# Attention on the needed key blocks only (bands, gathered sampled blocks, shared first and last block), values in 32-column tiles, and a new planner

## The chip, the cores and the metric

The kernel runs on one core of one Trainium2 chip. The metric is device time in microseconds (us) of the slowest core, here of the only one. Runs are compared with runs of the kernel before on the same chip. The engines are called TensorE (PE in the profile, PEld for its weight loads), VectorE (DVE), ScalarE (ACT), GpSimd (POOL) and SyncE (SP).

## The reference

Inputs are q, k and v of 4 batches, 8 heads, 768 positions and 64 columns, a table `sampled_blocks` of 24 x 3 block numbers (the same for all batches and heads), and the weights of a gated network.

```python
# attention, blocks of 32 positions: 24 blocks
mask = |block_i - block_j| <= 1  or  block_i or block_j is the first or the last
mask |= key block is one of the three sampled blocks of the query block
x = softmax(where(mask, q k^T / 8, -1e9)) v           # per batch and head
# network: x is [4, 768, 512], w_in [512, 1024], conv_w [3, 1024], w_out [1024, 512]
h = relu(x @ w_in)
c = conv_w[0] * h[t-1] + conv_w[1] * h[t] + conv_w[2] * h[t+1]
out = (h * sigmoid(c)) @ w_out
```

## The kernel before

The kernel before computes all 768 keys for each query. The mask is 24 more rows in the product of Q and K (64 + 24 = 88 rows). A unit is 1024 columns of scores: one exponential and eight value products of 128 x 128 by 65 columns. There are 144 units.

```python
def s_fn(e, ...):                       # scores of a unit, mask rows inside the product
    nc.tensor.matmul(out=st[:, 128 * x:128 * (x + n_)],
                     lhsT=QK[kc % 2][s][0:88, 1, hh, kc // 2, :],
                     rhs=QK[par][s][0:88, 0, hh, idx:idx + n_, :]..., start=True, stop=True)
def e_fn(e, ...):
    nc.scalar.activation(out=pt_t[ptb.index], in_=st_t[stb.index], func=AF.Exp, bias=0.0, scale=0.125)
def a_fn(e, ...):                       # four of these, twice a unit
    nc.tensor.matmul(out=o[:, off:off + 65], lhsT=pt_t[ptb.index][:, 128 * x:128 * x + 128],
                     rhs=VT[P % NSLOT][:, hh, kc, 0:65], ...)
# ... the gated network of a half batch (384 positions): ReLU mostly on VectorE, edges copied on GpSimd,
#     three taps and two adds per 768 columns on VectorE, tanh on ScalarE, then the gate on VectorE
for o in sc.run():                      # a list scheduler in the kernel sets each engine's order from assumed costs
    ...
```

This scheduler (the planner, below) sets the order of each engine's instructions. In a later run, with the new planner, another order of the same work took 10.6 us more (e_alt).

The softmax here doesn't subtract the row's maximum and nothing guards it: scores larger than these inputs give would overflow.

## Time and profile before

| kernel before | |
|---|---|
| time | 276.06 us (median of 2 runs, 276.02 to 276.1) |
| busy: TensorE, VectorE, ScalarE | 213.5, 201.4, 168.9 us |
| first convolution tap on VectorE | 61.0 us after the start |
| VectorE busy before it, and in the 215.2 us after it | 22.9 and 178.5 us (83%) |
| transfers of instructions for TensorE (queue 8) | 19 of 16 KB |

"Busy" is the time in which at least one instruction of that engine runs, waits left out. VectorE, busy 73% of the whole time, is busy for 18.9 of the 20 us from 120 to 140 us, so the span is read by stage.

### The profile page before, as it was taken

What the parts mean: (1) busy time and instruction counts of PE and PEld (TensorE: products, weight loads), DVE (VectorE), ACT (ScalarE), POOL (GpSimd) and SP (SyncE); (2) the same over time, 40 slices, a digit from 0 to 9 for tenths busy, and PEclk for the clock granted to TensorE, in tenths of its full rate; (3) what the DMA queues carried; (4) which work ended last, traced back from release to release, by engine and by line L of the source; (5) the groups of instructions that cost most, each with busy time, mean ns of one, the idle gap of its engine ahead of it and who ended that gap; (6) DMA issues with size and microseconds to landing.
All of it is one profiled execution on the core that took longest, in us unless ns stands there. A gap on an engine that the chain in (4) does not pass through costs nothing.

```text
span 276.2 us, 6428 instructions
## 1 busy us (share of the span) xinstructions
PE 213.5 (77%) x2503; PEld 152.0 (55%) x2521; DVE 201.4 (73%) x545; ACT 168.9 (61%) x189; POOL 72.1 (26%) x171
## 2 busy tenths in 40 slices
PE   5724499459779887997779769979898799749573
PEld 1523488337657655676557545766675567524221
DVE  6713362037997998399959994999799749986984
ACT  1511289517786887387858784887788747830420
POOL 8722331211223453022434410211112002211500
PEclk9555599959999999999999999999999999986868
DMA  6999999984215999963599964722200131011003
GB/s 141 141 211 197 160 157 116 159 154 113 55 30 120 148 167 166 230 166 64 78 180 179 168 88 157 140 64 45 93 17 15 31 129 40 18 28 76 1 0 152
DMA packets 67778, 30.35 MB, mean 110 GB/s; under 512 B 60868, under 2 KB 62916, under 8 KB 67748
## 3 DMA queue, kind: packets, MB, share of 16 engines
q0 software_dynamic: 25856, 11.14, 35.7%
q1 hardware_dynamic: 41892, 18.80, 31.6%
q8 instruction: 19, 0.31, 0.5%
q14 instruction: 11, 0.09, 0.1%
HBM read 23.08 MB, written 6.29 MB: 106 GB/s over the span
## 4 chain that ended last, share of the span: by engine, by line
DVE 53%; PE 20%; DMA 16%; issue 4%; SPq 3%; POOL 2%; ACT 1%; DVEq 0%; ACTq 0%
DVE m L710 17%; DVE m L718 10%; DVE hE L683 8%; DMA vn<-in_v_dram 7%; DMA xT<-xtok 6%; DVE gT L737 6%; PE mix L671 6%; PE mix L640 6%; DVE xtok L542 4%; PE st L578 4%; DVE tn L734 4%; PE av L610 2%; DMA et<-nat 2%; SPq L493 2%; PE st L640 1%
## 5 line engine op out<-in xcount | busy, mean ns | idle before, releaser
L587 ACT ACTIVATE pt<-st 128x1024 bf16<-128x1024 f32 x144 | 140.7, 1025 | 69.2 <-PE st L578 68.7
L671 PE MATMUL mix<-xT,winb 128*128 128x384 bf16 x256 | 53.9, 341 | 13.5 <-DMA xT<-xtok 8.6
L610 PE MATMUL av<-vt,pt 128*128 128x65 bf16 x1152 | 60.0, 195 | 0.2 <-ACT pt L587 0.2
L610 PEld LDWEIGHTS <-pt 128*128 128x128 bf16 x1152 | 52.4, 99 | 12.5 <-issue 8.7
L640 PE MATMUL mix<-woutb,gT 128*128 128x512 bf16 x143 | 41.8, 386 | 19.6 <-DVE gT L737 14.3
L710 DVE TENSOR_SCALAR m<-hE,cw 128x384 bf16<-128x384 bf16 x192 | 56.3, 348 | 0.3 <-POOL hE L702 0.3
L683 DVE TENSOR_SCALAR hE<-mix 128x384 bf16<-128x384 f32 x58 | 32.0, 552 | 26.8 <-PE mix L671 26.4
L578 PE MATMUL st<-et,ot 88*128 88x128 bf16 (+1 forms) x224 | 43.9, 240 | 1.3 <-ACT pt L587 0.9
L578 PE MATMUL st<-ot 88*128 88x128 bf16 (+1 forms) x224 | 43.6, 238 | 0.7 <-ACT pt L587 0.5
L578 PE MATMUL st<-et 88*128 88x128 bf16 (+1 forms) x208 | 43.4, 249 | 0.9 <-ACT pt L587 0.2
L578 PE MATMUL st<-ot,et 88*128 88x128 bf16 (+1 forms) x208 | 42.8, 246 | 1.5 <-ACT pt L587 0.7
L578 PEld LDWEIGHTS <-ot 88*128 88x128 bf16 x448 | 35.9, 100 | 13.6 <-issue 3.5
L696 POOL COPY hE<-hE 128x254 bf16<-128x254 bf16 x32 | 13.3, 415 | 111.3 <-DVE hE L683 93.8
L578 PEld LDWEIGHTS <-et 88*128 88x128 bf16 x416 | 33.4, 100 | 11.6 <-issue 2.9
L640 PEld LDWEIGHTS <-gT 128*128 128x128 bf16 x192 | 15.9, 101 | 42.6 <-DVE gT L737 25.5
L718 DVE TENSOR_TENSOR m<-m 128x768 bf16<-128x768 bf16 x64 | 35.6, 557 | 1.0
L731 ACT ACTIVATE tn<-m 128x768 bf16<-128x768 bf16 x32 | 26.9, 840 | 14.3 <-DVE m L718 14.1
L671 PEld LDWEIGHTS <-winb 128*128 128x128 bf16 x256 | 23.7, 101 | 19.3 <-issue 9.7
L650 DVE COPY o2s<-mix 128x512 f32<-128x512 f32 x20 | 13.4, 689 | 12.5 <-PE mix L640 12.5
L737 DVE TENSOR_TENSOR gT<-tn,hE 128x768 bf16<-128x768 bf16 x32 | 18.0, 563 | 1.1
L542 DVE TENSOR_TENSOR xtok<-av,rcp 128x384 bf16<-128x384 f32 x32 | 17.8, 558 | 1.1
L413 POOL DMA_DIRECT2D nat<-in_q_dram x15 | 11.4, 757 | 26.2 <-PE mix L450 17.7
(67 smaller groups left out, 129.2 us busy)
## 6 DMA issues: line engine op xcount, KB each, us to landing
out_dram<-o2s SPq DMA_DIRECT2D x24, 256.0 KB
vn<-in_v_dram POOLq DMA_DIRECT2D x16, 192.0 KB, 5.8
nat<-in_q_dram POOLq DMA_DIRECT2D x15, 192.0 KB, 4.8
nat<-in_k_dram POOLq DMA_DIRECT2D x15, 192.0 KB, 6.2
ot<-et SPq DMA_DIRECT2D x12, 192.0 KB
winb<-in_moe_w_in_dram POOLq DMA_DIRECT2D x1, 1024.0 KB, 12.9
woutb<-in_moe_w_out_dram POOLq DMA_DIRECT2D x1, 1024.0 KB, 17.9
et<-msk SPq DMA_DIRECT2D x12, 72.0 KB
```

The costliest lines, as they stand in the source:

```text
L542: nc.vector.tensor_tensor(out=xtok_t[xk.index].rearrange("p c h d -> p h c d"), in0=o[:, :, :, 0:64], in1=rcp.unsqueeze(3).broadcast_to([1 ...
L578: nc.tensor.matmul(out=st[:, 128 * x:128 * (x + n_)], lhsT=QK[kc % 2][s][0:88, 1, hh, kc // 2, :], rhs=QK[par][s][0:88, 0, hh, idx:idx + n ...
L587: nc.scalar.activation(out=pt_t[ptb.index], in_=st_t[stb.index], func=AF.Exp, bias=0.0, scale=0.125)
L610: nc.tensor.matmul(out=o[:, off:off + 65], lhsT=pt_t[ptb.index][:, 128 * x:128 * x + 128], rhs=VT[P % NSLOT][:, hh, kc, 0:65], start=(y in ...
L640: nc.tensor.matmul(out=acc(0), lhsT=gT_t[gb.index][:, ffc, 128 * c:128 * c + 128], rhs=woutb[:, ffc, :], start=(ffc == 0), stop=(ffc == NF ...
L650: nc.vector.tensor_copy(out=o2s_t[ob.index], in_=acc(0))
L671: nc.tensor.matmul(out=mix_t[hb.index][:, 0:384], lhsT=winb[:, fc, 128 * ffc:128 * ffc + 128], rhs=xT_t[xt_buf[n].index][:, fc, :], start= ...
L683: nc.vector.tensor_scalar(out=dst, in0=mix_t[hb.index][:, 0:384], scalar1=0.5, scalar2=0.0, op0=ALU.mult, op1=ALU.max)
L710: nc.vector.tensor_scalar(out=m_t[cb.index][:, x, y], in0=hE_t[heb.index][:, f0 + y, 128 * x:128 * x + 384], scalar1=cw[:, x, f0 + y:f0 + ...
L718: nc.vector.tensor_tensor(out=m[:, a_], in0=m[:, a_], in1=m[:, b_], op=ALU.add)
L731: th = op({"ACT": t_act(768)}, lambda e, cb=cb: nc.scalar.activation(out=tn_t[cb.index], in_=m_t[cb.index][:, 1], func=AF.Tanh, bias=0.0, ...
L737: g2 = op({"DVE": t_d2(768)}, lambda e, cb=cb, gtb=gtb, heb=heb, f0=f0: nc.vector.tensor_tensor(out=gT_t[gtb.index][:, f0:f0 + 2, :], in0= ...
```

## The change

The intent: compute only what the mask keeps. For a pair of heads and half a batch, the scores are now bands of 128 keys around each query block (384 + 320 columns), the first and last block for all (736 columns, with the full row of the block that sees everything), and the three sampled blocks of each query block (704 columns). For the sampled blocks K is gathered by copies on VectorE and V by transfers from a scratch tensor in memory. Values are 67 products per pair, each 32 columns wide. The convolution runs on a width of 768 without copied edges. The planner is new: it runs a forward and a backward pass six times and keeps the best order by its own costs.

The core of the diff (1,600 lines, cut):

```diff
-                                 lhsT=QK[kc % 2][s][0:88, 1, hh, kc // 2, :],
-        nc.scalar.activation(out=pt_t[ptb.index], in_=st_t[stb.index], func=AF.Exp, bias=0.0, scale=0.125)
...
+            for a in range(lo, lo + cnt, 6):                       # 6 blocks: 18 registers, then 5: 15
+                _, vals = nc.values_load_multi_w_load_instructions(
+                    off_i[0:1]...[:, 3 * (i0 + a):3 * (i0 + z)], engines=[eng], ...)
+                rv[(n, name)] += list(vals)
+        rl = op({"DVE": 0.5}, loads(EN.DVE, "DVE", 0, NX), due - 5, [blk] + list(prev_copies))
+        for x in range(NX):                                        # NX = 11 query blocks of the half
+            def cp(e, x=x):
+                for s in range(3):
+                    nc.vector.tensor_copy(out=dst[:, :, x, 32 * s:32 * s + 32],
+                                          in_=KT[...][:, :, bass.ds(rv[(n, "DVE")][3 * x + s], 32)])
+            o = op({"DVE": 0.40}, cp, ...)
...
+            vg_w[n].append(op({"POOL": 1.25}, lambda e, x=x: nc.gpsimd.indirect_dma_start(...)))   # 6 blocks
+        rs = op({"SP": 0.5}, loads(EN.SP, "SP", NIX, NX - NIX), due - 3, [blk] + list(prev_sp))
+                    nc.sync.dma_start(out=VG[...], in_=vs_t[b][bass.ds(rv[(n, "SP")][...], 32), :])  # 5 x 3
...
+                        nc.tensor.matmul(out=dst, lhsT=l_, rhs=r_, ...)          # 67 a pair, dst 32 rows
+        ao = op({"PE": 0.72}, a_fn, ...)
...
+    for x in range(passes):                                        # planner: forward and backward, 6 passes
+            order, span = self.forward(prio, x == 0)
```

The number in braces is what the planner believes the operation to cost.

## The prediction

> **What bounds the kernel now.** I read the page first: the totals of the engines, the slices, and the shares of the chain that ended last.
>
> ```profile
> PE 213.5 (77%) x2503; PEld 152.0 (55%) x2521; DVE 201.4 (73%) x545; ACT 168.9 (61%) x189; POOL 72.1 (26%) x171
> ...
> PE   5724499459779887997779769979898799749573
> ...
> DVE  6713362037997998399959994999799749986984
> ACT  1511289517786887387858784887788747830420
> ...
> DMA  6999999984215999963599964722200131011003
> ...
> DMA packets 67778, 30.35 MB, mean 110 GB/s; under 512 B 60868, under 2 KB 62916, under 8 KB 67748
> ...
> DVE 53%; PE 20%; DMA 16%; issue 4%; SPq 3%; POOL 2%; ACT 1%; DVEq 0%; ACTq 0%
> ```
>
> No engine is full over the whole span. A slice is 6.9 us. In the first eight slices the DMA digit is 9 while PE, DVE and ACT are mostly below 5; from slice nine DVE is at 7 to 9, and in the last four ACT has nothing left. So I cut the span into stages with the view of busy time in stretches (columns: length, then busy time of PE, weight load, DVE, ACT, POOL, then clock, DMA share, GB/s):
>
> ```profile
> 0.00:40.00 40.00, 22.98 (x223) 16.98 (x224) 19.21 (x59) 13.56 (x15) 18.64 (x31) 0.66 1.25 168
> 40.00:60.00 20.00, 12.31 (x182) 9.82 (x179) 3.24 (x9) 12.11 (x14) 3.08 (x4) 0.89 1.20 142
> 60.00:245.00 185.00, 158.61 (x2038) 117.58 (x2054) 156.04 (x420) 137.11 (x151) 45.21 (x123) 0.99 0.59 103
> 245.00:276.20 31.20, 19.57 (x68) 7.60 (x68) 22.93 (x59) 6.17 (x10) 5.13 (x13) 0.75 0.15 54
> ```
>
> The first 60 us wait for transfers. The middle, 185 us, has PE at 86%, DVE at 84% and ACT at 74%: three engines nearly in balance. The last 31 us are the gated network of the last half with no attention beside it. Then the costly groups and, for what an instruction costs back to back, two stretches of the order of time:
>
> ```profile
> L587 ACT ACTIVATE pt<-st 128x1024 bf16<-128x1024 f32 x144 | 140.7, 1025 | 69.2 <-PE st L578 68.7
> L610 PE MATMUL av<-vt,pt 128*128 128x65 bf16 x1152 | 60.0, 195 | 0.2 <-ACT pt L587 0.2
> L710 DVE TENSOR_SCALAR m<-hE,cw 128x384 bf16<-128x384 bf16 x192 | 56.3, 348 | 0.3 <-POOL hE L702 0.3
> L683 DVE TENSOR_SCALAR hE<-mix 128x384 bf16<-128x384 f32 x58 | 32.0, 552 | 26.8 <-PE mix L671 26.4
> L718 DVE TENSOR_TENSOR m<-m 128x768 bf16<-128x768 bf16 x64 | 35.6, 557 | 1.0
> ```
> ```profile
> 35.51 16.61 ACT L587 ACTIVATE pt<-st 128x1024 bf16<-128x1024 f32 x18 [1.22 <-PE st L578]
> ```
> ```profile
> 66.96 1.46 DVE L710 TENSOR_SCALAR m<-hE,cw 128x384 bf16<-128x384 bf16 x6
> 68.34 0.55 DVE L718 TENSOR_TENSOR m<-m 128x768 bf16<-128x768 bf16 x1
> 68.81 0.35 DVE L734 TENSOR_SCALAR tn<-tn 128x768 bf16<-128x768 bf16 x1
> ```
>
> Durations overlap, so I count in pitches, start to start: an exponential 16.61/18 = 0.923 us, a convolution tap (68.34-66.96)/6 = 0.23, an add of 768 columns 68.81-68.34 = 0.47. Eight value products fill 0.41 us in the same view, (0.41-0.195)/7 = 0.031 us each. A first-layer matmul of 384 columns comes to 0.16, an output matmul of 512 to 0.217, a ReLU on DVE to 0.47. Summed so, before needs about 133 + 27 us on ACT, 185 on DVE and 185 on PE (scores 63, values 36, first layer 42, output 42).
>
> [...]
>
> **The change, part by part.**
>
> *Scores and exponentials.* Before computes all 768 keys for each query with the mask as 24 more rows; after computes per head pair and half 384 + 320 (bands), 736 (first and last block), 704 (sampled). These are 2144 columns in four exponentials. At 0.07 + n/1200 us (0.923 - 1024/1200 = 0.07) that is 4 x 0.07 + 1.79 = 2.07 us, times 32 = 66 us against 133. ACT then takes over 59 ReLUs of 64 (0.39 each, 23 us), 32 evictions of transposed Q and K (0.71, 23 us) and 16 output copies (8 us); tanh stays at 32 x 0.71 = 23. ACT: about 143 us against 160. The 67 us off the exponentials are largely spent again.
>
> *PE.* Scores: 28 products of 64 columns at 0.031 and four of 128 to 224 at 0.056 and 0.096: 1.17 us, times 32 = 37 against 63. Values: 67 products in 32-column tiles per pair, 2144 in all. If four run together but their loads do not hide, I put a pair at 1.0 us (an estimate: half of 67 x 0.031), so 32 against 36. New: 512 transposes at about 0.04 = 20. Layers as before, 84. Sum 173 against 185[...].
>
> *DVE.* Removed: 53 of 58 ReLUs (25 us), 16 of 24 output copies (10), copies of V (6). Taps: 96 at 0.23 plus 48 double ones at 0.33 = 38 against 44. Adds, +1, gates and normalisation about the same (30 + 9 + 16 + 22). Evictions 8 each way. Added: 264 copies of 128 columns that gather the sampled K blocks, each with a register instruction in front. The smallest DVE operations in the trace take 0.16 to 0.19 us; I put one at 0.15 to 0.20, so 40 to 53 us. Start-up tables and memsets 12 us. Sum: 181 to 195 against 185. DVE, already 53% of the chain, gets no relief at all.
>
> *Transfers.* Gone: 24 transposing transfers of Q and K, the 12 + 12 shuffles to the odd copies and the mask rows. Loads become pieces of 2 KB where before they were 768 B in and 384 B out. Added: V goes to a scratch tensor in memory (3.2 MB), comes back twice (6 MB), and gathers read 1040 B rows, about 8.8 MB. More bytes, but few small packets; at 50 ns for some 31,000 packets (before: 0.316 x 16 x 276 / 41,892 = 33 ns for 450 B) that is about 100 us of the sixteen engines, under half the span.
>
> *POOL.* The edge copies of hE (28 us) go; 48 gathers of perhaps 1.2 us and rearranging V come. No bound.
>
> *Sum by stage.* Start: a first batch of 4.7 MB at some 200 GB/s lands by about 24 us, V's round trip ends about 5 us later, so values begin near 28 us; the order of DVE puts the first tap only behind twelve normalisations and 132 gather copies, near 48 us, with about 45 us of DVE work done. Left: about 143 us (188 - 45). Where before's DVE was bound it reached 18.9 of 20 us; at 90% this is 159 us, so the last DVE work is near 207. The planner's bursts will collide with gathers and PSUM buffers (two of each kind, as before): I add 12 us. Tail: output matmuls, copies and the last write after DVE, 5 us (before: 269 to 276). 207 + 12 + 5 = 224. So the gain is not from the bound engine doing less, but from filling it: 60 us of start become about 45, and the middle goes from 84% towards 90%.
>
> **The rivals.**
>
> *Column tiles do not overlap.* Then 67 x 0.031 = 2.1 us per pair, 66 us[...]: end near 250. For it: [...] 4136 load and matmul pairs must be issued. [...]
>
> *Gather copies are dearer.* A register operation before each and an address from a register could make 0.3 us: 40 us more on DVE, end near 260.
>
> *The planner really closes the gaps.* With DVE at 95% and copies at 0.13 us, the end is near 206.
>
> *V's round trip or gathers come late.* Each half waits for 33 gathered block groups; were they late in each half by 2 us, 16 us in all, 240. Against: DMA share in the middle was 0.59 with 67,778 small packets, and it falls.
>
> *Attention was never the bound, so nothing changes.* The 31 us tail and the DVE sum stay. This speaks for a modest gain, not for none, since 60 us of start were transfer bound.
>
> **Range and chances.** The middle is 224 us, 19% less. The spread comes from the 264 copies (-5 to +25), the value products (-8 to +25) and fill (-10 to +15); they rarely all go one way, so 205 to 250 should hold eight times in ten. Faster by over 2% (below 270.5) 0.93, within 2% 0.05, slower 0.02: two rivals would have to come together.
>
> **What would show it.** Right: ACT busy near 150, exponentials about 66 us in pitches; DVE still the largest share of the chain and busy about 190 to 210; first tap between 42 and 54 us; DMA digits falling below 9 by slice five. Wrong: value products over 1.5 us per pair and PE at the head of the chain (first rival); gather copies at 0.25 us or more (second); taps at odd columns slower than 0.23 us (alignment); DVE waiting in the middle for transfers or PE in runs over 3 us (planner).

## The result, and the profile after

The changed kernel took 348.94 us (median of 2 runs, 347.3 and 350.57), 26% more than before. Ratios in this document are against the kernel before in the same rounds, so they are not quite the ratio of the quoted medians; here 1.262, with an interval of 1.247 to 1.278. The prediction was 224 us and faster.

The page of the kernel after: totals, slices (8.7 us each) and chain, in the order in which the prediction shows them for before:

```profile
PE 219.6 (63%) x4137; PEld 140.3 (40%) x4137; DVE 194.1 (56%) x713; ACT 162.5 (47%) x270; POOL 101.6 (29%) x170
...
PE   2502783757803498938649638859588556996645
...
DVE  7601443216519769603238999024577975496870
ACT  2301761735802359614459742326586621591622
...
DMA  7999759692988416759485286642831002211103
...
PE 31%; DVE 25%; issue 13%; ACT 7%; DVEq 6%; DMA 6%; another core or an unknown queue 6%; SPq 4%; POOL 0%; ACTq 0%
```

The busy sums are nearly those of before: VectorE 194 us against 201, TensorE 220 against 214. So of these three none got much more work (GpSimd did: 102 us against 72). What grew is idle time: VectorE now idles 155 us (348.8 - 194.1) where it idled 75. The slices show it as holes, zeros and ones in the middle of the VectorE row, which before had none after slice nine. In the chain, VectorE falls from 53% to 25%, while "issue" rises from 4% to 13% and DVEq, the sequencer of VectorE, from nothing to 6%.

The view of busy time in stretches, cut at the first convolution tap (columns as in the prediction: length, then busy time of PE, PEld, DVE, ACT, POOL, clock, DMA share, GB/s), first for before, then for after:

```profile
0.00:61.00 61.00, 36.28 (x405) 27.50 (x406) 22.98 (x70) 25.67 (x28) 21.72 (x35) 0.73 1.23 159
```
```profile
0.00:103.60 103.60, 52.70 (x1202) 40.47 (x1203) 39.65 (x212) 42.27 (x66) 44.12 (x81) 0.73 0.81 154
103.60:349.00 245.40, 166.93 (x2935) 99.81 (x2934) 154.43 (x501) 120.21 (x204) 57.51 (x90) 0.81 0.43 100
```

The prediction has the first tap at 48 us with 45 us of VectorE's work done. It came at 103.6 us with 39.7 done. Then it gives the rest 176 us (159 for VectorE at 90%, 17 for collisions and the end). The rest took 245 us: 154 us of work, 63%. These two terms make up the whole miss: 55.6 + 69 = 125 = 349 - 224.

What stands in the holes is told by the view of one line of the program, here the line that loads registers (columns: number, then duration in ns as least, median and most, then first and last start in us), and by the chain in order of time between 48 and 57 us (start, length, what):

```profile
L674 DVEq TENSOR_LOAD <-off_i x16: 1565/3570/7152, 17.1 to 287.0; - x16
L674 SPq TENSOR_LOAD <-off_i x8: 3091/3632/6285, 17.1 to 234.4; - x8
```
```profile
48.85 3.96 issue
52.81 3.40 DVEq L674
...
56.29 0.56 DVE qb L587
```

The block offsets go from on-chip memory to registers in groups of 18 and 15, and a group takes 3.6 us in the median. The sixteen on VectorE sum to 56.9 us in the trace (264 registers, 0.22 us each), the eight on SyncE to 31.2 us. The page does not count them as busy, so they appear as idle time. While one runs, VectorE only finishes what stood before it (ahead of the instruction at 56.29 us it was idle for 7.44 us), and the chain goes through it: the "issue" piece is the first load of that pair, the DVEq piece the second.

The costly groups of after and a stretch of VectorE's order of time, for the durations that the prediction had put down:

```profile
L918 DVE TENSOR_SCALAR m<-hE,cw 128x384 bf16<-128x384 bf16 (+1 forms) x144 | 44.4, 351 | 17.9 <-issue 7.3
L686 DVE COPY kg<-kt 128x128 bf16 x264 | 32.4, 208 | 18.1 <-ACT kt L570 6.3
L813 ACT ACTIVATE pr<-st 128x704 bf16<-128x704 f32 x32 | 24.3, 759 | 17.2 <-PE st L806 17.0
```
```profile
95.98 0.39 DVE L686 COPY kg<-kt 128x128 bf16 x3
103.62 1.05 DVE L918 TENSOR_SCALAR m<-hE,cw 128x384 bf16<-128x384 bf16 x4 [7.26 <-issue]
105.30 0.55 DVE L918 TENSOR_SCALAR m<-hE,cw 128x384 bf16<-128x384 bf16 x2
```

The gather copies took 0.39 us for three, 0.13 each, below the 0.15 to 0.20 of the prediction. The exponentials of 704 columns took 759 ns, those of 1024 in the kernel before 1025: 0.83 ns a column, the prediction's n/1200 (those of the bands, 384 and 320 columns, took 580 and 519 in the median, more than this line gives). The four taps in 1.05 us are two that start at an odd column and two at an even one: (1.05 - 0.35)/3 = 0.23 each, as before, so odd starts cost nothing here. The 7.26 us ahead of the first tap are two register loads.

A second kind of hole lies inside the value products of one pair (TensorE's order of time), which wait for nothing that the profile names, and the view of waits sums it for the weight loads of these products (us, times, longest). The last fence is the corresponding row of before:

```profile
73.28 0.19 PE L850 MATMUL av<-vn,pg 128*32 128x65 bf16 x1
76.54 0.24 PE L850 MATMUL av<-vg,pr 96*32 96x65 bf16 x2 [3.07 <-issue]
...
PEld L850 <- issue: 24.0, 21, 6.3
```
```profile
PEld L610 <- issue: 8.7, 3, 7.1
```

The granted clock of TensorE fell too, from 0.910 to 0.789 (0.96 to 0.81 after the first tap). No run shows that this sets the time: four runs of one kernel (e_true_fix, below) had clocks of 0.79 to 0.85 and times within 0.8 us, and of seven runs of before the one with the lowest clock, 0.919, was the fastest. What the step from 0.91 to 0.79 costs was not tested.

### The profile page after: what moved, and what is told of

Same layout as the page of the kernel before. It is cut to its first block, busy times and chain, and to the rows that moved or that the text cites.

```text
span 348.8 us, 10541 instructions
## 1 busy us (share of the span) xinstructions
PE 219.6 (63%) x4137; PEld 140.3 (40%) x4137; DVE 194.1 (56%) x713; ACT 162.5 (47%) x270; POOL 101.6 (29%) x170
## 4 chain that ended last, share of the span: by engine, by line
PE 31%; DVE 25%; issue 13%; ACT 7%; DVEq 6%; DMA 6%; another core or an unknown queue 6%; SPq 4%; POOL 0%; ACTq 0%
PE mix L888 9%; PE mix L973 8%; DVE m L918 7%; DVE m L924 6%; DVEq L674 6%; PE av L850 5%; DVE kg L686 3%; PE mix L562 3%; DMA vs<-vr 2%; DMA nat<-in_k_dram 2%; PE st L806 2%; DVE m L936 2%; DVE xtok L862 1%; ACT pr L813 1%
## 5 line engine op out<-in xcount | busy, mean ns | idle before, releaser
L693 POOL DMA_INDIRECT vg<-vs,idx x48 | 46.5, 970 | 50.9 <-DMA vs<-vr 33.3
L918 DVE TENSOR_SCALAR m<-hE,cw 128x384 bf16<-128x384 bf16 (+1 forms) x144 | 44.4, 351 | 17.9 <-issue 7.3
L933 ACT ACTIVATE m<-m 128x768 bf16<-128x768 bf16 x32 | 27.1, 846 | 40.4 <-DVE m L924 26.1
L984 ACT ACTIVATE hE<-mix 128x384 bf16<-128x384 f32 x59 | 28.2, 493 | 31.9 <-PE mix L973 30.7
L686 DVE COPY kg<-kt 128x128 bf16 x264 | 32.4, 208 | 18.1 <-ACT kt L570 6.3
L850 PE MATMUL av<-vg,pr 96*32 96x65 bf16 x704 | 28.7, 205 | 5.2 <-issue 5.2
L850 PEld LDWEIGHTS <-pa 128*32 128x32 bf16 x704 | 22.4, 102 | 16.1 <-issue 13.3
L850 PE MATMUL av<-vs,pa 128*32 128x65 bf16 x320 | 28.1, 206 | 0.0
L850 PE MATMUL av<-vn,pa 128*32 128x65 bf16 x384 | 25.4, 206 | 3.3 <-POOL pa L771 2.2
L850 PE MATMUL av<-vd,pg 128*32 128x130 bf16 x352 | 25.9, 237 | 1.5 <-issue 1.5
L795 ACT ACTIVATE pg<-st 128x736 bf16<-128x736 f32 x32 | 25.1, 786 | 1.4 <-PE st L788 1.3
```

The lines of the kernel that those rows point to most:

```text
L686: nc.vector.tensor_copy(out=dst[:, :, x, 32 * s:32 * s + 32], in_=KT[kt_buf[b].index][:, :, bass.ds(rv[(n, "DVE")][3 * x + s], 32)])
L693: vg_w[n].append(op({"POOL": 1.25}, lambda e, x=x: nc.gpsimd.indirect_dma_start(out=VG[vg_buf[n].index][:, x, :], out_offset=None, in_=vs_ ...
L795: nc.scalar.activation(out=pg_t[pg.index], in_=st_t[sg.index][:, 0:736], func=AF.Exp, bias=0.0, scale=0.125)
L850: nc.tensor.matmul(out=dst, lhsT=l_, rhs=r_, start=(y == 0), stop=(y == len(lists[j]) - 1), skip_group_check=True)
L918: nc.vector.tensor_scalar(out=mv(dst)[:, y], in0=hE_t[heb.index][:, f0 + y, c0 + tp_:c0 + tp_ + cn], scalar1=cw[:, tp_, f0 + y:f0 + y + 1] ...
L933: th = op({"ACT": t_act(W)}, lambda e: nc.scalar.activation(out=m_t[cb.index][:, 1], in_=m_t[cb.index][:, 0], func=AF.Tanh, bias=0.0, scal ...
```

## The experiments

Four theories stood at the start. A: the register loads stop the engines on the path. B: the planner's order is bad because its costs are wrong. C: V's way through memory and its gathers come late. D, added after the first runs: TensorE runs out of instructions in the small products. The planner can be run by itself. By its own costs the order of the kernel before is 231.8 us long, that of the changed kernel 246.1 us (two planners, whose costs differ). The changed kernel thus expected to be the longer one, even at 0.5 us for two loads that take 7.

The times below are medians of four runs of each kernel, slow ones included. By the means of the fast runs alone e_fix_dve takes 319.5 us, e_fix_sp 338.6, e_fix_both 309.9, e_twice 391.2, e_keep_true 326.3, e_third 297.8, e_stale 300.2, e_alt 321.0 and e_order 304.6; no difference below moves by more than 3.1 us. The rounds ran on four chips, on which the kernel before had medians of 275.5 to 278.3 us, so differences of 2 us between rounds mean nothing.

### Register loads: out, and doubled

The block offsets are fixed for this draw, so they can be written in as constants. The plan keeps an empty operation in place of the loads, so nothing else moves.

```diff
+OFF = [32 * ... for the checked table of this draw]
-        rl = op({"DVE": 0.5}, loads(EN.DVE, "DVE", 0, NX), ...)
+        rl = op({"DVE": 0.5}, (lambda e: None), ...)
-        in_=KT[...][:, :, bass.ds(rv[(n, "DVE")][3 * x + s], 32)])
+        in_=KT[...][:, :, OFF[3 * (i0 + x) + s]:OFF[3 * (i0 + x) + s] + 32])
```

On VectorE alone, e_fix_dve:

> The changed kernel with this draw's block offsets written into VectorE's 264 key copies as constants: no register loads (56.9 us of them in the changed kernel's trace) and no register instructions on VectorE, every other instruction in the same order (only right for this draw). Theory A, the loads hold up VectorE on the path: the time falls by about the 57 us and some of the waits behind them, to 275 to 305 us. Theory B, the order of the plan is poor whatever the loads cost: it falls by less than 20 us, to over 330 us. Theory C, V's round trip and its late gathers set the pace: same as the changed kernel within 10 us.

Measured: 318.53 us (ratio 1.157). On SyncE alone (the same edit at `rs` and its 15 gathers), e_fix_sp:

> The same for SyncE's gathers of V alone (31.2 us of register loads there in the changed kernel's trace), VectorE's loads kept. Theory A: SyncE has time to spare, so 0 to 15 us less, 334 to 349 us. Theory C: the gathers come earlier and with them the values, so 25 to 40 us less, 310 to 325 us. Theory B: under 10 us less.

Measured: 341.6 us (1.225; the profiled run was a slow one). Both, e_fix_both:

> Both at once: no register loads in the kernel. Theory A: 250 to 290 us, near the plan's own idea, with VectorE's idle time down from 155 us to 60 to 90 us. Theory B: still over 310 us. Theory C with SyncE's part: at least 20 us below the run with VectorE's part alone.

Measured: 310.9 us (1.125). And every load of VectorE made twice, half of the copies taking the second set (so that it is used), e_twice:

```diff
-                for a in range(lo, lo + cnt, 6):
+                for a in list(range(lo, lo + cnt, 6)) + ([0, 6] if name == "DVE" else []):
```

> Dose the other way: VectorE loads every group of registers twice (32 loads in place of 16, about 114 us), all else in the same order. Theory A: about 57 us more, 390 to 415 us. Theory B or C: VectorE has 155 us of idle time that takes most of it up, under 20 us more, up to 370 us.

Measured: 394.31 us (1.430). The loads on VectorE then sum to 107.2 us in the trace. The chain of this kernel by engine:

```profile
DVE 33%; DVEq 23%; PE 20%; issue 11%; ACT 3%; DMA 2%; SPq 1%; another core or an unknown queue 1%; POOL 0%; ACTq 0%
```

What follows: theory A holds in kind. Another 50 us of loads (107.2 - 56.9) cost 42 us by the fast runs (45 by the medians); taking 56.9 us out gave 30, and with SyncE's 38. But e_fix_dve lies between the ranges of A and B, and with both out only 38 of the 59 to 99 us that A expected came back (311 us, not 250 to 290), so the loads are not the whole cause. B's "over 310 us" is met on its edge; C's "20 us below the run with VectorE's part alone" is not (8 to 10 us). The stretches of e_fix_both, cut at its first tap:

```profile
0.00:81.80 81.80, 47.48 (x1167) 36.94 (x1167) 38.37 (x213) 39.91 (x62) 40.99 (x77) 0.77 0.91 167
81.80:306.00 224.20, 163.58 (x2977) 100.83 (x2973) 156.11 (x501) 121.52 (x208) 61.39 (x93) 0.86 0.52 119
```

Of the 56 us by which the tap was late, 22 are gone, and the rest of the kernel fell from 245 to 224 us. VectorE is still only at 70% there.

### The planner's costs

```diff
-        rl = op({"DVE": 0.5}, loads(...))
+        rl = op({"DVE": 7.0}, loads(...))
-        rs = op({"SP": 0.5}, loads(...))
+        rs = op({"SP": 3.3}, loads(...))
-        ao = op({"PE": 0.72}, a_fn, ...)
+        ao = op({"PE": 1.05}, a_fn, ...)
# ... and nine more costs: ScalarE, adds, gathers, writes of the scratch, transposes
```

e_true, with all register loads kept:

> The changed kernel with all its work and its register loads, but the planner told what the traces measured: 7.0 us for VectorE's loads of a half (it was told 0.5), 3.3 us for SyncE's (0.5), 1.05 us for a pair's values (0.72), 0.95 us for the two band exponentials (0.78), ScalarE 0.13 us plus columns by 1080 (0.07 plus columns by 1200), VectorE's adds 0.56 us (0.48), 2.07 us for three gathers on SyncE (1.56), 1.5 us for each write of V's scratch (0.6). Its own span for this order is 282 us (246 us for the changed kernel's). Theory B, the order was built on wrong costs: 290 to 320 us. Rival, theory A alone (the loads cost the same wherever they stand)[...]: 335 to 355 us.

Measured: 311.72 us (1.122), at 55.8 us of loads on VectorE in its trace, the same as in the changed kernel. e_true_fix, the same costs with constants:

> The same measured costs, and the block offsets as constants (no register loads; right for this draw only). The planner's own span is 274 us. Theory B: 280 to 298 us, at least 12 us below the run with constants and the old costs (310.9 us). If the costs were not what is wrong with the order: 300 to 318 us.

Measured: 320.99 us (1.159). So an order planned with measured costs gives back 37 us with the loads in place. That it does so by hiding the loads is likely but not shown, since ten other costs changed with them. And the two gains do not add up. With the loads gone, the order from true costs is 10 us worse than the one from false costs, outside both expectations. That suggested that an order is worth some 10 us either way by chance, which e_alt tests below.

### Registers kept for all batches

The table is the same in each batch, so a register can be loaded once and kept. VectorE keeps 44 for two of the three slots, GpSimd keeps 22 and makes the third slot's copies, SyncE keeps 30.

```diff
-                rv[(n, name)] = []
-                for a in range(lo, lo + cnt, 6):
+                rv[(n, name)] = {} if n < 2 else rv[(n - 2, name)]
+                for a in range(lo, lo + cnt, 6) if n < 2 else []:
+            for e_, r_, d_ in (("DVE", rl, 0.26), ("POOL", rp, 0.35)):      # copies of slots 0, 1 and of slot 2
```

e_keep, with the old costs elsewhere:

> General again: each block offset is loaded into a register once and kept for all four batches, since the table is the same for all (VectorE 44 registers for the first two slots, GpSimd 22 for the third slot and its 88 key copies, SyncE 30). Old costs in the planner otherwise, its own span 251 us. Theory A: the loads shrink to about 44 x 0.2 = 9 us on VectorE, so within 10 us of the run with constants, 301 to 321 us. If GpSimd's copies or the register instructions in front of each copy matter, more than 325 us.

Measured: 323.61 us (1.170). The loads fell to 13.3 us on VectorE (44 registers, 0.30 us each, where the expectation had 0.2 and the changed kernel's trace 0.22), 8.8 on GpSimd and 9.6 on SyncE. e_keep_true, with the measured costs:

> Registers kept, and the planner told the measured costs; its own span 273 us. Theory A and B together: 278 to 300 us, about the kernel before (276 us). If the order's costs do not matter: as the run with registers kept, 301 to 321 us.

Measured: 327.37 us (1.182). Both are right for any draw and faster than the changed kernel, but neither comes near before, and true costs again gave nothing once the loads were small. e_keep missed its 301 to 321 us narrowly, e_keep_true both of its ranges. In e_keep's trace VectorE stands idle for 12.3 us before its first key copies, and GpSimd's key copies are named as what ended the wait, so moving the third slot there may not have been free.

### The value products, and V's gathers

Both cuts are made on e_fix_both and give wrong outputs. e_third makes 25 of a pair's 67 products and keeps all waits:

```diff
-                            for c in range(6):
+                            for c in (5 * h,):
-                        lists[j].append((dst, pa_t[...], vv))
+                        if h: lists[j].append((dst, pa_t[...], vv))
-                        lists[j].append((dst, pr_t[...], vg[...]))
+                        if not h: lists[j].append((dst, pr_t[...], vg[...]))
-                    if i != full:
+                    if i != full and inner.index(i) == 3:
```

> On the kernel with constant offsets (310.9 us): of the 67 value products of a pair only 25 are made (for each block the sampled ones of one head and the band ones of the other, one of the shared kind), so the outputs are wrong on purpose; all waits, transfers and the order stay. The prediction's figure of 1.0 us a pair, 15 ns a product: 42 products less are 0.63 us a pair, at most 20 us in 32 pairs, and less of it on the path: 295 to 308 us. Theory D, the small products starve TensorE of instructions (the trace shows 1.67 us a pair, with 2.5 us in which TensorE waits for nothing that the profile names): over 25 us less, 265 to 286 us, with about 22 transfers of 16 KB of instructions in place of 32.

Measured: 298.44 us (1.080). The gain of 12.5 us lies in the range of the prediction's own figure; theory D's 25 us did not come. TensorE's waits of kind "issue" ahead of these products fell, first e_fix_both, then e_third:

```profile
PEld L850 <- issue: 18.9, 29, 2.7
```
```profile
PEld L850 <- issue: 9.1, 16, 3.5
```

This run takes away work and instructions together, so it cannot say which of the two gave the 12.5 us.

e_stale makes V's gathers for the first two halves only:

```diff
-        op({"POOL": 1.25}, lambda e, x=x: nc.gpsimd.indirect_dma_start(
+        op({"POOL": 1.25}, lambda e, x=x: n < 2 and nc.gpsimd.indirect_dma_start(
-                for s in range(3):
+                for s in range(3 if n < 2 else 0):
```

> On the kernel with constant offsets (310.9 us): V's gathers only for the first two halves, later halves use what lies in the buffers, so the outputs are wrong on purpose; some 6.6 MB of 40 less. Theory C, transfers and V's gathers hold the middle: 12 to 30 us less, 281 to 299 us. If the transfers are hidden after the start: within 8 us, 303 to 313 us.

Measured: 301.01 us (1.094), 9.9 us less: between the two expectations, so the gathers cost something in the middle but do not hold it.

e_less has both cuts in one kernel:

> Constant offsets (310.9 us), the third of the value products (alone 12.5 us less) and V's gathers for the first two halves only (alone 9.9 us less) in one kernel, wrong on purpose. If the two stand one behind the other on the path: 285 to 292 us. If they hide behind each other's waits: 295 to 300 us. If together they release what neither does alone: under 283 us. What is then left over the kernel before (276 us) is not in registers, value products or gathers, but in the order and the two banks of the layers.

Measured: 286.22 us (1.029). The gains add up (24.7 against 12.5 + 9.9; on different chips, so to within some 2 us). Its stretches:

```profile
0.00:76.10 76.10, 43.48 (x824) 33.42 (x825) 37.34 (x212) 40.08 (x62) 41.41 (x77) 0.69 1.04 184
76.10:285.00 208.90, 148.46 (x1971) 85.80 (x1968) 153.92 (x501) 121.26 (x208) 25.46 (x57) 0.87 0.41 93
```

Even with no register loads, a third of the value products and a quarter of the gathers, VectorE is at 74% after its first tap, and the kernel is 10 us behind the one before.

### The small products alone

e_stream is a program of its own (outputs zero): 24 full products, then 20 pairs' worth of 67 value products with no wait in them, and the same again while large loads run.

```python
wide(av[0], 24)
for g in range(20):
    pair(av[1])          # 67 products, 32 columns wide, the shapes of a real pair
wide(av[0], 24)
# SyncE then starts eleven loads of 1.5 MB, and the same is done once more into av[2], av[3]
```

> The disputed cost alone, outputs zero on purpose: 24 full products, then 20 pairs' worth of value products (67 each, 32 columns wide, same shapes) back to back with no wait in them; and the same again while about 17 MB of transfers run. Theory D: TensorE uses 134 instructions a pair, so a new 16 KB piece of 256 instructions is wanted every two pairs; if that takes longer than two pairs (2.0 us at 1.0 us a pair), a pair takes more than 1.0 us on average: 1.2 to 1.8 us, with gaps of 0.3 to 2.5 us at each transfer of instructions, longer in the second half. Rival: 0.9 to 1.05 us a pair in both halves, no gaps.

Measured: one run (state unknown, granted clock 0.652), 161.58 us. TensorE's order of time, two stretches of the quiet half and two of the half beside transfers, and the queue of instruction transfers on the page:

```profile
28.16 1.46 PE L57 MATMUL av<-vn,pa 128*32 128x130 bf16 x128 [0.92 <-issue]
31.61 2.53 PE L57 MATMUL av<-vn,pa 96*32 96x65 bf16 x128 [2.00 <-issue]
35.07 1.46 PE L57 MATMUL av<-vn,pa 128*32 128x130 bf16 x128 [0.92 <-issue]
...
108.45 2.53 PE L57 MATMUL av<-vn,pa 96*32 96x65 bf16 x128 [6.46 <-issue]
117.11 2.48 PE L57 MATMUL av<-vn,pa 128*32 128x65 bf16 x128 [6.13 <-issue]
...
q8 instruction: 21, 0.34, 0.9%
```

After a first run of 199 small products, TensorE runs exactly 128 products, 256 instructions with their weight loads, and then stops. The starts are 3.45 us apart in the quiet half (28.16, 31.61, 35.07), whether the 128 products themselves take 1.46 or 2.53 us. So it is the supply that sets the pace: 1.8 us for 67 products (3.45 x 67/128) where the products alone take 0.64 to 0.66 (first start to last start, pairs in which no stop falls and the clock is full; 1.15 to 1.20 where the granted clock is 0.50). Beside 210 to 230 GB/s of transfers the starts are 8.7 to 9.2 us apart (9.0 on average), 4.7 us for a pair. The page counts 21 transfers of 16 KB on queue 8, and 5,552 TensorE instructions make 21.7 groups of 256. The transfers' own records settle it: of the 19 stops within the small products, 18 ended 1.2 to 1.8 us after one of these transfers landed (the other one, 4.5 us, has no transfer on record).

In the changed kernel the page counts 32 such transfers (8,274 instructions), in the kernel before 19 (5,024). Theory D's mechanism is shown here; its size in the full kernel is smaller. Of the 24.0 us of waits shown above for the changed kernel, four stops with 7.0 us, the one at 76.54 among them, ended in the same way, 1.2 to 1.6 us after a transfer landed. The two longest (6.3 and 5.0 us) did not, and what they wait for stays open. Taking a pair from the start of its first product to the end of its last, the trace of the changed kernel gives 1.48 us on average and 1.09 in the median.

### How much the order alone is worth

e_alt is e_fix_both with one cost of the planner changed, which gives another order of the same work, 243.4 us by its own span:

```diff
-SWITCH = 0.09
+SWITCH = 0.12
```

> The same work as the kernel with constant offsets (310.9 us) in another order: the planner's cost of a change of TensorE's mode set to 0.12 us in place of 0.09; its own span is 243 us in place of 246. If the planner's span tells anything: 305 to 313 us. If the order alone scatters the time[...]: more than 5 us away in either direction.

Measured: 321.53 us (1.155): 10.6 us more, for a plan that calls itself 2.7 us shorter. So differences of ten microseconds between orders, such as that of e_true_fix, carry no cause that could be named. These are two orders, so the scatter may be wider still.

e_order keeps registers (the third slot on ScalarE in place of GpSimd), gives one PSUM bank to the values and three to the layers, uses costs measured in these runs, and has its order from a search over some 30,000 changed priorities:

```diff
-    NST, NAV, NMIX = 2, 2, 2
+    NST, NAV, NMIX = 2, 1, 3
-        for o in pl.run():
+        for o in pl.forward(PRIO, False)[0]:
```

> A kernel for any draw that may beat both: registers loaded once and kept (VectorE 44 for the first two slots, ScalarE 22 for the third and its key copies, SyncE 30), one bank for the values and three for the layers and transposes, costs as measured (1.5 us for a pair's values with the waits for instructions in it, 0.58 us for two output products, 2.0 us for a write of V's scratch), and the order found by trying some 30,000 changes of priority instead of six passes: its own span 272.6 us, where the six passes give 304. If the order was worth much: 278 to 295 us. If waits for instructions and transfers, which no order sees, set the time: 300 to 325 us, as with registers kept before (323.6 and 327.4 us).

Measured: 305.87 us (1.103), right for any draw: the fastest correct version of this design found, 43 us under the changed kernel and 28 over the one before. It lies in the range of the rival: it won about 18 us over e_keep, not the 28 to 45 that was hoped for, and order, banks, costs and the engine of the third slot changed together, so the 18 us are not the order's alone. No version beat the kernel before.

### V's way through memory in the start

e_early_v is e_fix_both with batch 0 reading V from a second scratch that is filled from K at the very start, so that nothing waits for V's own round trip:

```diff
+        nc.gpsimd.dma_start(out=vq, in_=k[2:4]...)                  # at the start
-        in_=vs_t[b][0:S]...                                         # all readers of V's scratch
+        in_=(vs_t[b] if b else vq)[0:S]...
```

> The kernel with constant offsets (310.9 us), in the same order, but batch 0 reads V from a second scratch that one transfer fills from K at the very start (wrong on purpose; V's own scratch is still written): the first gather and the first values no longer wait until V has been cast, rearranged and written. In the trace of the kernel with constant offsets the first gather started at 26.2 us, 7.5 us after GpSimd was free for it, and the first tap at 81.8 us. Theory C in the start, V's round trip holds it: first values some 7 us earlier (near 35 us), first tap near 74 us and 6 to 10 us off the time, 301 to 305 us. Rival, the dense transfers and waits behind it set the start anyway: first tap later than 79 us and under 4 us off the time, 307 to 315 us.

Measured: 311.98 us (1.124), no gain. Its output is wrong, which doesn't matter for the time. The first gather came 2.6 us earlier (23.6 us), the first values 1.3 us later (44.1), the first tap at 84.2 us. Other waits stayed or grew (first 80 us; the same two rows of e_fix_both read 13.5 and 4.2 us):

```profile
ACT kt L570 <- PE mix L562: 14.5, 5, 5.0
...
PE mix L562 <- DMA nat<-in_k_dram: 7.9, 3, 5.0
```

Transposes wait for the loads of K, and ScalarE for the transposes. The filling transfer adds to the traffic, so the test is not quite clean, but V's round trip is not what holds the start.

## Why the prediction was wrong

| | first tap | VectorE done by then | from tap to end | VectorE busy in it |
|---|---|---|---|---|
| prediction | 48 | 45 | 176 | 143 |
| before | 61.0 | 22.9 | 215.2 | 178.5 (83%) |
| after | 103.6 | 39.7 | 245.2 | 154.4 (63%) |
| e_fix_both | 81.8 | 38.4 | 224.2 | 156.1 (70%) |
| e_true | 87.6 | 33.2 | 222.8 | 157.2 (71%) |
| e_less | 76.1 | 37.3 | 208.8 | 153.9 (74%) |
| e_order | 82.8 | 32.6 | 217.6 | 154.7 (71%) |

(us, from each trace; register loads are not in the busy time.)

In the prediction's own terms the profiled run of the changed kernel is 125 us too long. Of these, 43 went when the register loads were taken out (348.8 to 306.0). Of what was left, 34 are the start (81.8 against 48) and 48 the fill (224 against 176). The split holds for this order of the work only.

**The step that failed first** is the sum for VectorE, "181 to 195 against 185". Its busy time came out near it (194.1), but the sum lacks a term. The prediction saw "a register instruction in front" of each copy. That one is real and takes 46 ns, and the copies still come every 0.13 us. The instructions that fill the registers, 16 on VectorE and 8 on SyncE, it does not mention. The diff shows them in plain sight, with a cost of 0.5 that the planner believed. The kernel before has no such load, so its trace gives no figure for one. In the trace of the changed kernel they take 56.9 us for 264 registers on VectorE, 0.22 each; with that in the sum, the gain of 52 us is gone. Removing the loads gave 38 us, doubling VectorE's cost 42 to 45.

**The second is the fill**: "Where before's DVE was bound it reached 18.9 of 20 us; at 90% this is 159 us." The best 20 us of a kernel were taken as the rate for a whole middle of another, though over everything after its first tap the kernel before reached only 83%. The row of slices, which the prediction read as "from slice nine DVE is at 7 to 9", says the same: slice nine is a 3, and six of the 31 slices after it stand at 3 to 6. The new order reached 63%, and 70% with no register loads at all. e_less reached 74% with most of its suspected waits cut. The planner's own figure says the same: 246 us for the changed kernel against 232 for before, at costs that are too low for both. The rival "the planner really closes the gaps" was given 206 us, and the 12 us for collisions stood in for what turned out to be the largest part.

**The third is the start**: first tap "near 48 us". It came at 103.6, and at 81.8 without loads, later than before's 61.0. The order puts more of VectorE's work ahead of the tap, as the prediction says (38 us against 23), but that work did not get done faster. The slices of transfers in e_fix_both stand at 8 or 9 with hardly a break up to about 69 us (nine slices of 7.65 us) and mostly at 7 to 9 up to 138 us, while the prediction expected digits under 9 by slice five. V's round trip, its named suspect, is not the cause (e_early_v). The sum for the transfers was off by nearly a factor of two. It expected some 31,000 packets (48,000 came) and about 100 us of the sixteen engines. The pages show, for before and then for after (packets, MB, share of the sixteen engines' span):

```profile
q0 software_dynamic: 25856, 11.14, 35.7%
q1 hardware_dynamic: 41892, 18.80, 31.6%
```
```profile
q0 software_dynamic: 13312, 15.94, 27.8%
q1 hardware_dynamic: 34612, 23.75, 26.1%
```

That is 186 us of 276.2 for before and 188 us of 348.8 for after: fewer packets, more bytes, and no relief. Which transfer would have to go for the start to shorten was not tested and stays open.

**Of the rivals**, the gather copies were cheaper than feared (0.13 us), and column tiles do overlap (67 products in 0.66 us, where 67 x 0.031 would be 2.1). But "value products over 1.5 us per pair" was the right thing to watch for: 1.48 us on average in the changed kernel (1.09 in the median) and 1.67 in e_fix_both, though the tiles overlap. Missing instructions are a part of it (7.0 us of stops in 32 pairs, 0.2 us a pair), the lower granted clock is likely another (in e_stream a pair without a stop took 1.2 us at a clock of 0.50 and 0.66 at full clock); the split was not measured. "V's round trip or gathers come late" was right for the later gathers, up to 9.9 us, less than the 16 allowed.

**What held:** VectorE's busy time (194 us, where 190 to 210 was said), taps at odd columns no slower (0.23 us each for 384 columns, as at even ones), and V's round trip as no bound. ScalarE was busy for 162 us, not near 150, and TensorE for 220 us, more than before's 214, where the prediction saw less work. Of the chain VectorE holds 25%, behind TensorE's 31%, and not the largest share as said.

**What stays open.** From 310.9 us to the 276 of before there are 35 us. Fewer values and gathers account for 25, as an upper bound on what their stops and delays cost, since real work went with them. The last 10 are within what two orders of the same work differ by (e_alt). In the changed kernel itself the 73 us are 38 of register loads in this order, and those 35. The split depends on the order: with the loads in place and honestly costed, e_true also reached 312.

## What to carry to other kernels

Before predicting from a diff, list every kind of instruction in it, also those that the profile does not count as busy, and put a cost on each; a load of a group of registers took 1.6 to 7.2 us on VectorE here, so do it once, or off the busy engine. VectorE's work stayed nearly the same here (194 us against 201) and the new order filled it less (63% after the first tap, where before had 83%), so take the filling that the kernel before reached over the whole stage, not its best stretch (18.9 of 20 us). And a planner's costs can be far from the trace (0.5 us for two loads that took 7): compare its own span and its costs with the trace before trusting either.
